# Softmax-weighted causal taps and a soft mixture of experts on one core: taps loaded to every row they need, logits steps and conv heads each in a row

## The chip, the core and the metric

The kernel runs on one core of one Trainium2 chip, in fp32. The metric is the device time of one execution in microseconds (us). The core has TensorE (PE; its weight loads are listed as PEld), VectorE (DVE), ScalarE (ACT), GpSimd (POOL), SyncE (SP, which issues nearly all transfers here) and 16 DMA engines. A name with a q (SPq, ACTq) is the queue of that engine.

## The reference, cut to what matters

```
w = softmax(weight, axis=-1)                   # 8 heads x 7 taps
x_pad = 6 zero rows before each of the 8 sequences of 3584 x 192
out[b,s,h*24:(h+1)*24] = sum_k w[h,k] * x_pad[b,s+k,h*24:(h+1)*24]
X = out.reshape(28672, 192)
logits = X @ phi                               # 32 slots: 8 experts x 4
d = softmax over the 28672 rows;  slot_in = d.T @ X
slot_out[e] = relu(slot_in[e] @ w1[e]) @ w2[e]   # 192 -> 1024 -> 192
c = softmax over the 32 slots;    result = c @ slot_out
```

## The kernel before, in words

**Batches and stages.** The 8 sequences ("batches" b0 to b7) go through in four units of two. `load_x(b)` brings a batch to one of five buffers (`rb0` to `rb4`) in nine transfers on SP's queue (L271, L275). Each buffer row block needs 8 halo rows copied inside the buffer (`halo`, L199, mostly on POOL). For b0 and b1 a quarter's halo is copied in two pieces, as it is for the last quarter of b2; otherwise a quarter is one copy. The buffer of b5, b6, b7 is that of b0, b1, b2, so their loads are added right behind `dispatch(0)`, `dispatch(1)`, `dispatch(2)`, which read it last.

**Conv.** `conv` multiplies a batch by banded matrices `toep`, one per head (L460). For b0 to b2 (below `NHB`) a batch goes in two halves of four calls with two heads each; from b3 on one call takes one head of the whole batch. Every call takes the next of four pairs of PSUM banks (`take`), skipping the two that `logits` holds, and is evicted into the buffer by ACT (L197), for even batches from b2 on by ACT or DVE. `turn` transposes 32 channels at a time on DVE (L504) into `xt`.

**Logits, dispatch.** `logits(unit)` is six `step`s (k = 0 to 5, L549), each reading the transposes k of both batches. `done` then adds the moves from PSUM on DVE (L575, a running minimum) and the exponentials on ACT (L590). `turn_d(b)` transposes the exponentials on PE (L615) and copies them back, and `dispatch(b)` (L640) adds the batch to the slot sums.

**End.** Slot inputs go through `w1` (L870) and `w2` (L912), the result `so` is gathered (L948, L951), and the outputs are multiplied out (L983), evicted (L197, L201) and stored (L1009). `rows(b)` (L667 to L684) makes the softmax over slots; its steps have priorities of 1000 and more and are fitted into gaps. The weights come in as 16 transfers for `w1` (half h=0 into `rb3`, behind `dispatch(3)`; half h=1 into `rb4`, behind `dispatch(4)`) and eight for `w2` (into `xt` and `rb0`), all on SP's queue (L296).

**Order.** Nothing runs in the order of the text. `Plan.order` simulates the engines with hand-set costs and priorities and then emits every engine's instructions in the order that it found; PE's steps carry `chain=True` and so keep the order in which they are added. `stage(b, s, between)` adds a batch's convs and takes a table of what is to be added ahead of which head. Before the change that table spread the logits steps and the `turn_d`s:

```python
    lead = (2, 1, 1, 2)
                ld = (3, 1, 1, 1) if j == 2 else lead
                for h, n in enumerate(ld):
                    between[h] = [lambda z=z: step(z) for z in range(k, k + n)]
            if s and j > 1:
                between = {0: [lambda: turn_d(prev[0])], 1: [lambda: turn_d(prev[1])], 2: [lambda: dispatch(prev[0])]}
            if b == B - 1:
                between.update({6: [lambda: box.extend(logits(unit)), lambda: box[0](0)], 7: [lambda: box[0](1)]})
```

**Start.** The 56 tap weights come to one row; a matmul with a row of ones (L346) spreads them to 128 rows in PSUM, DVE and ACT make the softmax, `tprod`, `tsum` and 16 small matmuls (`tmm`, L395) make the bands, and `tcp` (L405) copies them to `toep`. `warmup` (L337) and `filler` (L490) are matmuls whose results nobody reads.

Of the kernel before, what the change touches and what calls it, by code (L numbers as in the profile page):

```python
# [10 lines left out]
ALU = mybir.AluOpType  # L11
# [140 lines left out]
def tile_conv_softmoe(ctx: ExitStack, tc: tile.TileContext, x, weight, phi, w1, w2, out):  # L152
    nc = tc.nc
    P = 128
# [65 lines left out]
    dnx = sb("dnx", P, U, P)  # L220
    wb = sb("wb", P, H * KT)
    ident = sb("ident", P, P)
# [4 lines left out]
    acc = sb("acc", P, D)  # L227
    ones = acc[:, 0:P]
    dtot = sb("dtot", P, 1)
# [18 lines left out]
    odd2 = small[:, 6:8]  # L248
    wm, ws = small[:, 8 : 8 + H], small[:, 16 : 16 + H]
    hk = [[f"h{i}.{h}" for h in range(H)] for i in range(NR)]  # L250
# [5 lines left out]
    def load_x(b):  # L256
        i = b % NR
        pr = b * 10 - 30
        n = NU // NQ4

        def zero(e):
            nc.gpsimd.memset(rb[i][0 : 2 * HR, 0, :], 0.0)

        add(zero, {"POOL": 0.4}, writes=[f"z{i}"], after=allk(i) + [f"z{i}"], prio=pr)
        for q in range(NQ4):

            def fn(e, q=q):
# [12 lines left out]

            add(fn, {"DMA": n * P * D * 4 / 325e3 + {(0, 0): 0.6, (1, 1): 1.1}.get((b, q), 0)}, writes=[ldk[i][q]], after=hk[i] + [hak[i][q], hak2[i][q]], prio=pr)
            reads = [ldk[i][q]] + ([f"z{i}"] if q == 0 else [])
            if b < 2 or (b, q) == (2, 3):
                um = n * q + n // 2
                first = lambda e, q=q, um=um: halo(e, n * q, um)
                add(first, {"POOL": 0.75}, reads=reads, writes=[hak[i][q]], prio=pr)
                add(lambda e, q=q, um=um: halo(e, um, n * (q + 1)), {"ACT" if b == 0 and q < 2 else "POOL": 0.75}, reads=reads, writes=[hak2[i][q]], prio=pr)
            else:
                add(halo, {"POOL": 1.5}, reads=reads, writes=[hak[i][q]], prio=pr)
# [4 lines left out]
    def load_w(dst, src, nbytes, key, after, prio, depth=0, behind=None, first=False):  # L294
# [14 lines left out]
    wv = wb.rearrange("p (h k) -> p h k", k=KT)  # L309
    wrow = tap.rearrange("p h t -> p (h t)")[0:1, 0 : H * KT]  # L310
    add(
        lambda e: nc.scalar.dma_start(wrow, bass.AP(weight.tensor, 0, ap=[[0, 1], [1, H * KT]])),
        {"ACT": 2.4}, writes=["wrow"], prio=-100,
# [5 lines left out]
    def c0(e):  # L319
        nc.vector.memset(warm, 0.0)  # L320
        nc.scalar.activation(warm, warm, AF.Exp)
        make_identity(nc, ident)
        nc.gpsimd.memset(ones[0:1], 1.0)
        nc.gpsimd.memset(strip, 0.0)
# [9 lines left out]
    def warmup(n):  # L334
# [8 lines left out]

    warmup(1)
    add(
        lambda e: nc.tensor.matmul(prs[1][:, 0, 0 : H * KT], ones[0:1], wrow, start=True, stop=True),  # L346
        {"PE": 0.2}, reads=["wrow", "ident"], writes=["p1"], prio=-100, chain=True,
    )
    warmup(2)

    def w_max(e):
        wp = prs[1][:, 0, 0 : H * KT].rearrange("p (h k) -> p h k", k=KT)
        nc.vector.tensor_reduce(out=wm, in_=wp, axis=AX.X, op=ALU.max)
        nc.vector.tensor_tensor(out=wv, in0=wp, in1=wm.unsqueeze(2).broadcast_to((P, H, KT)), op=ALU.subtract)

    def w_norm(e):
        nc.vector.tensor_reduce(out=ws, in_=wv, axis=AX.X, op=ALU.add)
        nc.vector.tensor_scalar(out=ws, in0=ws, scalar1=1e-9, scalar2=None, op0=ALU.add)
        nc.vector.reciprocal(ws, ws)
        nc.vector.tensor_tensor(out=wv, in0=wv, in1=ws.unsqueeze(2).broadcast_to((P, H, KT)), op=ALU.mult)  # L360

    add(w_max, {"DVE": 0.5}, reads=["p1"], writes=["wb"], prio=-50)
    add(lambda e: nc.scalar.activation(wb, wb, AF.Exp), {"ACT": 0.25}, reads=["wb"], writes=["wb", "wexp"], prio=-50)
# [5 lines left out]
    add(w_norm, {"DVE": 0.9}, reads=["wb"], writes=["wb"], prio=-50)  # L369
    
    TB = 7
    KB = TB + KT - 1
    spread = dnx.rearrange("p u n -> p (u n)")[0:KB, 0 : H * TB * KT]

    def tprod(e):
        dst = spread.rearrange("p (h t k) -> p h t k", h=H, t=TB)
        eye = bass.AP(ident.tensor, ident.offset, ap=[[ident.ap[0][0], KB], [0, H], [1, TB], [1, KT]])
        nc.vector.tensor_tensor(out=dst, in0=eye, in1=wv[0:KB].unsqueeze(2).broadcast_to((KB, H, TB, KT)), op=ALU.mult)

# [5 lines left out]
    add(tprod, {"DVE": 0.45}, reads=["ident", "wb"], writes=["spread"], prio=-45)  # L385
    add(tsum, {"DVE": 0.45}, reads=["spread", "p1"], writes=["tap"], prio=-45)

# [28 lines left out]

    add(selector, {"DVE": 0.8}, reads=["ident"], writes=["gsel"], prio=1050)

# [4 lines left out]

    add(masks, {"DVE": 0.3}, reads=["ident"], writes=["mask"], prio=1050)

# [7 lines left out]

    add(row_parity, {"DVE": 0.6}, reads=["ident"], writes=["pmask"], prio=1051)

# [75 lines left out]
    def stage(b, s, between=()):  # L511
        between = dict(between)
        if b < NHB:
            spare = ((0, 0, 0, 4), (0, 0, 0, 1), (), (), (), ())
            for lo in (0, NI):
# [170 lines left out]
    for b in range(NR):  # L686
        load_x(b)
    lead = (2, 1, 1, 2)
    for j, unit in enumerate(units):
        prev = units[j - 1] if j else []  # L690
        for s, b in enumerate(unit):
# [4 lines left out]
            elif j == 1 and s == 0:  # L696
                for k in range(3):
                    lead0[0](k, 1)
                for k in range(3, NB):
                    lead0[0](k)  # L700
                lead0[1]()
                between = {
                    H: [lambda: state.update(held=())],
                    2 * H - 4: [lambda: turn_d(prev[0])],
                    2 * H - 2: [lambda: turn_d(prev[1])],
                }
            elif s == 0 and prev:
                step, done = logits(prev)
                k = 0
                ld = (3, 1, 1, 1) if j == 2 else lead  # L710
                for h, n in enumerate(ld):
                    between[h] = [lambda z=z: step(z) for z in range(k, k + n)]
                    k += n
                between[len(ld) - 1] += [done, lambda: dispatch(units[j - 2][1]), lambda: state.update(held=())]
            if s and j > 1:
                between = {0: [lambda: turn_d(prev[0])], 1: [lambda: turn_d(prev[1])], 2: [lambda: dispatch(prev[0])]}
            if b == B - 1:
                box = []
                between.update({6: [lambda: box.extend(logits(unit)), lambda: box[0](0)], 7: [lambda: box[0](1)]})
            stage(b, s, between)  # L720
            if b == 0:
                add(phi_copies, {"ACT": 1.05}, reads=["phi0", hk[0][6] + ".0"], writes=["phi4"], prio=12)
            if s == 0 and j == 1:
                dispatch(prev[0])
    step, done = box
    for k in range(2, NB):
        step(k)
# [317 lines left out]
```

## Time and profile before

| | |
|---|---|
| median of 3 runs | 200.6 us (200.0 to 201.22) |
| the profiled execution | 201.81 us, of which the span is 199.9 us |
| PE, DVE, ACT, POOL busy | 84%, 72%, 52%, 40% of the span |
| granted PE clock, mean | 0.93 |

The span begins with the first instruction and ends with the last transfer; 1.9 us of the execution lie around it. The profiled execution is 1.2 us above the median.

### The profile page before, as it was taken

To read this page: it belongs to the slowest core of one execution; us is meant where nothing else is said; L and a number is where in the kernel's file an instruction comes from. 1 tells how busy PE (TensorE), PEld (TensorE's weight loads), DVE (VectorE), ACT (ScalarE), POOL (GpSimd) and SP (SyncE) were. 2 spreads that over 40 slices of the span, in tenths; PEclk is the share of its full clock that TensorE was granted. 3 is DMA by queue.
4 is the path that set the end of the run, shared out by engine and by line. 5 is a ranking of instruction groups with operands and counts; after the bars stand their busy time and mean duration, and the time that the engine had idled before them with its cause. 6 is when DMAs were issued, how large, how long until landed. Compare 5 with 4: busy or idle time off the path is not lost.

```text
span 199.9 us, 6456 instructions
## 1 busy us (share of the span) xinstructions
PE 168.2 (84%) x2686; PEld 107.8 (54%) x2686; DVE 144.3 (72%) x242; ACT 104.7 (52%) x206; POOL 79.1 (40%) x79
## 2 busy tenths in 40 slices
PE   7996799989999999999999998997999998670000
PEld 3474646466434564355634584346999998660000
DVE  6568357579996989989999876588988998760000
ACT  3375343464924867428762450135999999560000
POOL 8364657556666056580004303327234345300000
PEclk9999699999999999999999999999999998867555
DMA  5999999999993899915897999920899999999994
GB/s 161 324 313 328 319 327 323 329 318 328 322 329 94 249 334 302 331 36 160 282 326 248 304 369 377 372 99 3 237 355 386 408 405 412 412 398 411 417 415 166
DMA packets 46767, 60.11 MB, mean 301 GB/s; under 512 B 2322, under 2 KB 39570, under 8 KB 46738
## 3 DMA queue, kind: packets, MB, share of 16 engines
q1 hardware_dynamic: 46528, 59.68, 88.7%
q8 instruction: 21, 0.34, 0.7%
q14 instruction: 8, 0.07, 0.1%
q10 hardware_dynamic: 210, 0.02, 0.1%
HBM read 37.68 MB, written 22.02 MB: 299 GB/s over the span
## 4 chain that ended last, share of the span: by engine, by line
PE 67%; DVE 7%; SPq 5%; DMA 4%; ACT 3%; issue 1%; POOL 0%; ACTq 0%; DVEq 0%
PE ps L460 20%; PE bk L983 16%; PE ps L549 13%; PE ps L640 10%; DMA rb<-in_x_dram 4%; SPq L275 4%; PE ps L615 4%; PE ps L870 3%; DVE rms L674 2%; ACT rb L197 2%; DVE eb L684 2%; ACT xt L590 1%; DVE eb L575 1%; DVE eb L677 1%; PE ps L897 1%
## 5 line engine op out<-in xcount | busy, mean ns | idle before, releaser
L504 DVE STREAM_TRANSPOSE xt<-rb 128x512 f32<-128x512 f32 (+1 forms) x66 | 58.1, 928 | 10.6 <-ACT rb L197 9.3
L199 POOL COPY rb<-rb 8x1536 f32<-8x1536 f32 (+1 forms) x39 | 46.6, 1197 | 36.2 <-DMA rb<-in_x_dram 33.4
L197 ACT COPY rb<-ps 128x768 f32<-128x768 f32 x57 | 43.0, 811 | 32.5 <-PE ps L460 29.2
L460 PE MATMUL ps<-rb,toep 64*64 64x192 f32 (+1 forms) x704 | 49.2, 415 | 3.5 <-POOL rb L199 2.8
L667 POOL TENSOR_TENSOR eb<-eb,rms 128x896 f32<-128x896 f32 x16 | 27.1, 1698 | 39.2 <-DVE rms L671 27.1
L983 PE MATMUL bk<-so,eb 32*128 32x192 f32 x448 | 38.9, 441 | 2.9 <-DVE eb L684 2.3
L983 PEld LDWEIGHTS bk<-so,eb 32*128 32x128 f32 x448 | 37.8, 317 | 3.7 <-issue 2.0
L460 PEld LDWEIGHTS ps<-rb,toep 64*64 64x64 f32 x704 | 25.4, 138 | 24.9 <-issue 12.8
L197 ACT COPY rb<-bk 128x384 f32<-128x384 f32 (+1 forms) x91 | 32.9, 505 | 5.3 <-PE bk L983 4.6
L549 PE MATMUL ps<-xt,phi 32*32 32x448 f32 x768 | 27.0, 544 | 0.1
L201 DVE COPY rb<-bk 128x384 f32<-128x384 f32 (+1 forms) x37 | 16.5, 490 | 4.1 <-PE bk L983 2.4
L549 PEld LDWEIGHTS ps<-xt,phi 32*32 32x32 f32 x768 | 10.3, 103 | 13.5 <-issue 6.8
L674 DVE TENSOR_REDUCE rms<-eb 128x28 f32<-128x896 f32 x16 | 17.1, 1069 | 0.5 <-ACT eb L680 0.5
L640 PE MATMUL ps<-rb,xt 128*32 128x192 f32 x320 | 13.8, 327 | 0.0
L590 ACT ACTIVATE xt<-eb,nmr 128x896 f32<-128x896 f32 x8 | 8.3, 1044 | 10.0 <-DVE eb L575 9.6
L640 PEld LDWEIGHTS ps<-rb,xt 128*32 128x32 f32 x320 | 10.0, 110 | 3.9 <-issue 1.2
L197 ACT COPY xt<-ps 128x512 f32<-128x512 f32 (+2 forms) x10 | 5.0, 517 | 9.5 <-DVE xt L201 8.6
L615 PE MATMUL ps<-ident,xt 128*128 128x128 f32 x64 | 8.7, 279 | 1.2 <-ACT rb L197 0.8
L615 PEld LDWEIGHTS ps<-ident,xt 128*128 128x128 f32 x64 | 6.9, 141 | 4.7 <-ACT xt L590 1.3
L684 DVE STREAM_TRANSPOSE eb<-eb 128x896 f32<-128x896 f32 x8 | 8.8, 1105 | 0.7 <-POOL eb L667 0.7
L677 DVE STREAM_TRANSPOSE eb<-eb 128x896 f32<-128x896 f32 x8 | 8.6, 1080 | 0.0
L640 PE MATMUL ps<-rb,dnx 128*32 128x192 f32 x192 | 8.4, 328 | 0.0
(98 smaller groups left out, 120.2 us busy)
## 6 DMA issues: line engine op xcount, KB each, us to landing
rb<-in_x_dram SPq DMA_DIRECT2D x56, 384.0 KB, 6.9
out_dram<-rb SPq DMA_DIRECT2D x28, 672.0 KB, 9.6
rb<-in_moe_w_dram SPq DMA_DIRECT2D x8, 512.0 KB, 4.8
xt<-in_moe_w_dram SPq DMA_DIRECT2D x4, 768.0 KB, 9.0
rb<-in_moe_w_dram SPq DMA_DIRECT2D x4, 768.0 KB, 12.0
rb<-in_x_dram SPq DMA_DIRECT2D x8, 288.0 KB, 6.1
rb<-in_moe_w_dram SPq DMA_DIRECT2D x8, 256.0 KB, 4.0
out_dram<-rb SPq DMA_DIRECT2D x4, 480.0 KB, 4.9
```

What stands on the lines that cost most here:

```text
L197: nc.scalar.copy(dst, src)
L199: nc.gpsimd.tensor_copy(dst, src)
L201: nc.vector.tensor_copy(dst, src)
L460: nc.tensor.matmul(dst[:, :, h * CG : (h + 1) * CG], toep[r, h0 + h, :], rb[i][r, lo + g : lo + n : 2, ch], start=True, stop=True,)
L504: nc.vector.transpose(xt[:, s, k, lo : lo + n], rb[i][:, lo : lo + n, 32 * k : 32 * k + 32])
L549: marks[f"L{unit[-1]}"] = nc.tensor.matmul(q[a % 2][32 * c : 32 * c + 32, a // 2, 0 : m * U * TH].rearrange("p (s u j) -> p s u j", s=m, j ...
L615: nc.tensor.transpose(q[:, u // 4, (u % 4) * P : (u % 4 + 1) * P], t[:, u].rearrange("p g t -> p (g t)"), ident)
L640: nc.tensor.matmul(q[32 * c : 32 * c + 32, 0, 0:D], d[:, u, 32 * c : 32 * c + 32], rb[i][:, U * c + u, :], start=(u == 0), stop=(u == U - 1),)
L667: return lambda e: veng(e).tensor_tensor(out=ev, in0=ev, in1=rb_, op=op)
L674: return lambda e: nc.vector.tensor_reduce(out=rm, in_=ev, axis=AX.X, op=op)
L684: add(lambda e: nc.vector.transpose(fl, fl), {"DVE": dve(NC)}, reads=ks, writes=[f"ct{b}"], prio=pr)
L983: nc.tensor.matmul(banks[own[c]][:, (q - k) * D : (q - k + 1) * D], cb[:, :, q], so[sl, :], start=True, stop=True, tile_position=(32 * c, 0),)
```

## The change

The tap weights are loaded to 13 rows at once, so the spreading matmul and its row of ones go, and the softmax works on 13 rows out of SBUF. The three warmups then stand in a row, and four fillers instead of one follow the second half of b0. Three small set-up steps on DVE wait for the bands. The last quarter of b3 gets its halo in two pieces. All six logits steps of a unit are added in a row; `dispatch` of the unit before's second batch follows them, and then the eight heads in a row. Both `turn_d`s stand ahead of the odd batch's heads (for unit 0: behind all of b2's), and `dispatch(prev[0])` behind that batch's heads.

```diff
-    wb = sb("wb", P, H * KT)
+    wb = sb("wb", P, H * KT)[0 : KT + 6]
-    ones = acc[:, 0:P]
...
-            if b < 2 or (b, q) == (2, 3):
+            if b < 2 or b < 4 and q == 3:
...
-    wrow = tap.rearrange("p h t -> p (h t)")[0:1, 0 : H * KT]
+    TB = 7
+    KB = TB + KT - 1
+    wrow = tap.rearrange("p h t -> p (h t)")[0:KB, 0 : H * KT]
     add(
-        lambda e: nc.scalar.dma_start(wrow, bass.AP(weight.tensor, 0, ap=[[0, 1], [1, H * KT]])),
+        lambda e: nc.scalar.dma_start(wrow, bass.AP(weight.tensor, 0, ap=[[0, KB], [1, H * KT]])),
...
-        nc.gpsimd.memset(ones[0:1], 1.0)
...
-    warmup(1)
-    add(
-        lambda e: nc.tensor.matmul(prs[1][:, 0, 0 : H * KT], ones[0:1], wrow, start=True, stop=True),
-        {"PE": 0.2}, reads=["wrow", "ident"], writes=["p1"], prio=-100, chain=True,
-    )
-    warmup(2)
+    warmup(3)
...
-    add(w_max, {"DVE": 0.5}, reads=["p1"], writes=["wb"], prio=-50)
+    add(w_max, {"DVE": 0.5}, reads=["wrow"], writes=["wb"], prio=-50)
...
-    add(selector, {"DVE": 0.8}, reads=["ident"], writes=["gsel"], prio=1050)
+    add(selector, {"DVE": 0.8}, reads=["ident", "toep7"], writes=["gsel"], prio=1050)
...
-            spare = ((0, 0, 0, 4), (0, 0, 0, 1), (), (), (), ())
+            spare = ((0, 0, 0, 4), (0, 0, 0, 4), (), (), (), ())
...
-                between = {
-                    H: [lambda: state.update(held=())],
-                    2 * H - 4: [lambda: turn_d(prev[0])],
-                    2 * H - 2: [lambda: turn_d(prev[1])],
-                }
+                between = {H: [lambda: state.update(held=())]}
             elif s == 0 and prev:
                 step, done = logits(prev)
-                k = 0
-                ld = (3, 1, 1, 1) if j == 2 else lead
-                for h, n in enumerate(ld):
-                    between[h] = [lambda z=z: step(z) for z in range(k, k + n)]
-                    k += n
-                between[len(ld) - 1] += [done, lambda: dispatch(units[j - 2][1]), lambda: state.update(held=())]
+                for k in range(NB):
+                    step(k)
+                done()
+                dispatch(units[j - 2][1])
+                state["held"] = ()
             if s and j > 1:
-                between = {0: [lambda: turn_d(prev[0])], 1: [lambda: turn_d(prev[1])], 2: [lambda: dispatch(prev[0])]}
-            if b == B - 1:
-                box = []
-                between.update({6: [lambda: box.extend(logits(unit)), lambda: box[0](0)], 7: [lambda: box[0](1)]})
+                between = {0: [lambda: turn_d(prev[0]), lambda: turn_d(prev[1])]}
             stage(b, s, between)
...
             if s == 0 and j == 1:
+                turn_d(prev[0])
+                turn_d(prev[1])
+            if j and s == (j > 1):
                 dispatch(prev[0])
-    step, done = box
-    for k in range(2, NB):
+    step, done = logits(unit)
+    for k in range(NB):
         step(k)
     done()
```

## Rows read from the trace of the kernel before

**Rows 1.** The page: 40 slices of 5 us; the chain's shares by engine.
```profile
PEclk9999699999999999999999999999999998867555
GB/s 161 324 313 328 319 327 323 329 318 328 322 329 94 249 334 302 331 36 160 282 326 248 304 369 377 372 99 3 237 355 386 408 405 412 412 398 411 417 415 166
...
PE 67%; DVE 7%; SPq 5%; DMA 4%; ACT 3%; issue 1%; POOL 0%; ACTq 0%; DVEq 0%
```
**Rows 2.** The chain in order of time: start us, us, what.
```profile
11.25 8.82 DMA rb<-in_x_dram
```
**Rows 3.** Timeline of PE to 25 us: start us, us, engine, line, operation, tile.
```profile
3.37 0.67 PE L346 MATMUL ps<-tap,acc 1*128 1x56 f32 x2
...
12.68 1.99 PE L490 MATMUL ps<-ident 128*128 128x256 f32 x8
...
17.46 0.70 PE L490 MATMUL ps<-ident 128*128 128x256 f32 x2
21.00 4.51 PE L460 MATMUL ps<-rb,toep 64*64 64x192 f32 x64 [2.84 <-POOL rb L199]
```
**Rows 4.** One window, all engines: us, busy by engine, PEclk, DMA share, GB/s.
```profile
22.00:23.00 1.00, 1.00 (x18) 0.84 (x16) 0.06 (x1) 0.80 (x1) 0.52 (x2) 0.50 1.11 300
```
**Rows 5.** Timeline of PE, the output stage.
```profile
167.28 4.86 PE L983 MATMUL bk<-so,eb 32*128 32x192 f32 x56 [0.64 <-DVE eb L684]
```
**Rows 6.** Timeline of PE, first logits steps to `dispatch(0)`.
```profile
25.44 2.48 PE L549 MATMUL ps<-xt,phi 32*32 32x448 f32 x48
27.85 1.53 PE L460 MATMUL ps<-rb,toep 64*64 64x192 f32 x32
...
42.32 1.03 PE L615 MATMUL ps<-ident,xt 128*128 128x128 f32 x8 [0.81 <-ACT rb L197]
...
45.93 2.81 PE L640 MATMUL ps<-rb,xt 128*32 128x192 f32 x64
```
**Rows 7.** Timeline of PE, b3 to the last logits step and `dispatch(5)`.
```profile
48.67 5.39 PE L460 MATMUL ps<-rb,toep 64*64 64x384 f32 x64
53.99 3.10 PE L549 MATMUL ps<-xt,phi 32*32 32x448 f32 x96
57.02 0.88 PE L460 MATMUL ps<-rb,toep 64*64 64x384 f32 x8
...
110.48 2.81 PE L640 MATMUL ps<-rb,dnx 128*32 128x192 f32 x64
```
**Rows 8.** Timeline of DVE, moves of unit 0 to the transposes of b3.
```profile
36.99 0.62 DVE L575 TENSOR_SCALAR_CACHE_REDUCE eb<-ps 128x448 f32<-128x448 f32 x1 [3.51 <-PE ps L549]
...
49.23 9.83 DVE L504 STREAM_TRANSPOSE xt<-rb 128x512 f32<-128x512 f32 x11
58.98 1.07 DVE L677 STREAM_TRANSPOSE eb<-eb 128x896 f32<-128x896 f32 x1
```
**Rows 9.** Timeline of POOL: last halo of b3, last halo of b7.
```profile
44.29 1.46 POOL L199 COPY rb<-rb 8x1536 f32<-8x1536 f32 x1 [1.27 <-DMA rb<-in_x_dram]
...
86.95 1.46 POOL L199 COPY rb<-rb 8x1536 f32<-8x1536 f32 x1 [0.71 <-DMA rb<-in_x_dram]
```
**Rows 10.** Timeline of SP's queue: load of b7, `w1` half h=1, output stores.
```profile
72.96 0.34 SPq L271 DMA_DIRECT2D rb<-in_x_dram  x1
...
100.40 1.84 SPq L296 DMA_DIRECT2D rb<-in_moe_w_dram  x3
...
139.18 49.33 SPq L1009 DMA_DIRECT2D out_dram<-rb  x36
```
**Rows 11.** End of the weight loads: one window of PE and DMA; PE's timeline.
```profile
131.00:132.00 1.00, 1.00 (x16) 1.00 0.37 138
...
133.91 0.49 PE L912 MATMUL ps<-xt 128*32 128x384 f32 x2
```
**Rows 12.** Timeline of ACT: the evictions of b3's eight heads.
```profile
49.65 5.72 ACT L197 COPY rb<-ps 128x768 f32<-128x768 f32 x8 [2.57 <-PE ps L460]
```
**Rows 13.** One window of the last stage, as in Rows 4.
```profile
180.00:190.00 10.00, 0.00 (x0) 0.00 (x0) 0.00 (x0) 0.00 (x0) 0.00 (x0) 0.60 1.02 412
```

More of the change, by code (lines that the diff above doesn't have):

```diff
@@ L248, in tile_conv_softmoe @@
     odd2 = small[:, 6:8]
-    wm, ws = small[:, 8 : 8 + H], small[:, 16 : 16 + H]
+    wm, ws = small[0 : KT + 6, 8 : 8 + H], small[0 : KT + 6, 16 : 16 + H]
     hk = [[f"h{i}.{h}" for h in range(H)] for i in range(NR)]
@@ L342, in warmup @@
             )
-    warmup(1)
-    add(
-        lambda e: nc.tensor.matmul(prs[1][:, 0, 0 : H * KT], ones[0:1], wrow, start=True, stop=True),
-        {"PE": 0.2}, reads=["wrow", "ident"], writes=["p1"], prio=-100, chain=True,
-    )
-    warmup(2)
+    warmup(3)
     def w_max(e):
-        wp = prs[1][:, 0, 0 : H * KT].rearrange("p (h k) -> p h k", k=KT)
+        wp = wrow.rearrange("p (h k) -> p h k", k=KT)
         nc.vector.tensor_reduce(out=wm, in_=wp, axis=AX.X, op=ALU.max)
-        nc.vector.tensor_tensor(out=wv, in0=wp, in1=wm.unsqueeze(2).broadcast_to((P, H, KT)), op=ALU.subtract)
+        nc.vector.tensor_tensor(out=wv, in0=wp, in1=wm.unsqueeze(2).broadcast_to((KB, H, KT)), op=ALU.subtract)
     def w_norm(e):
@@ L359, in w_norm @@
         nc.vector.reciprocal(ws, ws)
-        nc.vector.tensor_tensor(out=wv, in0=wv, in1=ws.unsqueeze(2).broadcast_to((P, H, KT)), op=ALU.mult)
-    add(w_max, {"DVE": 0.5}, reads=["p1"], writes=["wb"], prio=-50)
+        nc.vector.tensor_tensor(out=wv, in0=wv, in1=ws.unsqueeze(2).broadcast_to((KB, H, KT)), op=ALU.mult)
+    add(w_max, {"DVE": 0.5}, reads=["wrow"], writes=["wb"], prio=-50)
     add(lambda e: nc.scalar.activation(wb, wb, AF.Exp), {"ACT": 0.25}, reads=["wb"], writes=["wb", "wexp"], prio=-50)
@@ L377, in tprod @@
         eye = bass.AP(ident.tensor, ident.offset, ap=[[ident.ap[0][0], KB], [0, H], [1, TB], [1, KT]])
-        nc.vector.tensor_tensor(out=dst, in0=eye, in1=wv[0:KB].unsqueeze(2).broadcast_to((KB, H, TB, KT)), op=ALU.mult)
+        nc.vector.tensor_tensor(out=dst, in0=eye, in1=wv.unsqueeze(2).broadcast_to((KB, H, TB, KT)), op=ALU.mult)
     def tsum(e):
@@ L385, in tile_conv_softmoe @@
     add(tprod, {"DVE": 0.45}, reads=["ident", "wb"], writes=["spread"], prio=-45)
-    add(tsum, {"DVE": 0.45}, reads=["spread", "p1"], writes=["tap"], prio=-45)
+    add(tsum, {"DVE": 0.45}, reads=["spread"], writes=["tap"], prio=-45)
     def tmm(e):
@@ L422, in masks @@
             nc.vector.tensor_reduce(out=mask[:, a : a + 1], in_=src, axis=AX.XY, op=ALU.add)
-    add(masks, {"DVE": 0.3}, reads=["ident"], writes=["mask"], prio=1050)
+    add(masks, {"DVE": 0.3}, reads=["ident", "toep7"], writes=["mask"], prio=1050)
     def row_parity(e):
@@ L432, in row_parity @@
             )
-    add(row_parity, {"DVE": 0.6}, reads=["ident"], writes=["pmask"], prio=1051)
+    add(row_parity, {"DVE": 0.6}, reads=["ident", "toep7"], writes=["pmask"], prio=1051)
     state = {"pair": 0, "held": ()}
```

3 lines of the change are left out of this document (removed).

## The prediction, made before the changed kernel was built

> **What bounds the kernel now.** I read the chain first: PE holds 67% of it [rows 1]. Read in order of time it has three parts. To 21 us it is SP's issues and the landing of x: one piece of 8.82 us is nothing but b1's load [rows 2], and the conv of b1 starts at 21.00 behind the halo that waited for it [rows 3]. From 21 us to about 137 us it is PE. From then on it is the output: SP issues the stores from 139.18 on [rows 10], the transfers run at about 400 GB/s [rows 1], and between 180 and 190 us no engine computes while DMA is full at 412 GB/s [rows 13]. So the last part has a fixed length, as long as the outputs keep ahead of the queue, and whatever PE gains between 21 and 137 us arrives at the end. The second view is PE's timeline, which shows that PE hardly idles in that stretch but runs in three ways that cost: at half clock, waiting for ACT, and switching between kinds of matmuls. The third is DVE's timeline, which shows how little slack the transposes have behind it.
>
> **The change, part by part.** *Taps.* The spreading matmul (0.67 us [rows 3]) and a memset go. The bands are ready some tenths earlier, and that is worth nothing: the b1 load holds the chain until 21.00 whatever happens before it [rows 2, 3]. The same load covers the three set-up steps on DVE that move behind the bands, and the three more fillers: four fillers took 1.99 us and one 0.70 [rows 3], so PE ends at 17.46 + 1.99 = 19.45 instead of 18.16, still ahead of 21.00. Price of all this: nothing.
>
> *Clock at 21 us.* Before, PE sat idle for 2.84 us and then ran the four conv calls of b1's first half in 4.51 us [rows 3], at a granted clock of 0.50, which is 1.2 GHz [rows 4]. The slice 20 to 25 us is the only one before the output stage that shows less than 9 tenths [rows 1]. The fillers cut the idle time to 21.00 - 19.45 = 1.55 us. The trace has gaps on both sides of it: after 0.81 us at 41.5 us the clock stayed [rows 1, 6], after 0.64 us at 166.6 us it fell [rows 1, 5], but that was among matmuls on 32 of the 128 rows, and here the gap follows fillers on all 128 [rows 3, 5]. I take it that the clock holds. Then the four calls take about 2 x 1.53 = 3.06 us [rows 6] and end at 24.06; the three half logits steps behind them took 27.85 - 25.44 = 2.41 [rows 6], so b1's second half starts at about 26.45 instead of 27.85. That is 1.4 us; bounds 0 (the clock falls as before) and 1.45 (all that the four calls lose, 4.51 - 3.06).
>
> *b2 and `turn_d`.* Before, PE waited 0.81 us at 41.5 us for the exponentials and an eviction, then ran turn_d, a call, turn_d, a call, and reached `dispatch(0)` at 45.93: 4.42 us [rows 6]. With both calls first nothing waits for the exponentials: two calls at 1.53 / 2 and two turns at 1.03 [rows 6] are 3.59 us. Gain 0.8; bounds 0 (the calls wait for banks that ACT, busy with exponentials, has not emptied) and 0.8.
>
> *Rows of steps and heads.* A head alone between other matmuls takes 0.88 us, eight in a row 5.39, or 0.67 each [rows 7]. From 53.99 to 110.48 PE does 18 logits steps, 32 heads (b4 to b7), four turns and four dispatches, in 56.49 us [rows 7]. In a row, three steps cost 57.02 - 53.99 = 3.03, eight heads 53.99 - 48.67 = 5.32, a dispatch 48.67 - 45.93 = 2.74 [rows 6, 7], a turn 1.03. New sum: 6 x 3.03 + 4 x 5.32 + 4 x 2.74 + 4 x 1.03 = 54.54. Gain 1.95; bounds 0 (each row waits elsewhere for as much) and 1.95.
>
> Together 1.4 + 0.8 + 1.95 = 4.15 us. What is late next takes some of it back:
>
> *Transposes ahead of logits(2,3).* DVE goes from the first move at 36.99 to the end of b3's transposes at 49.23 + 9.83 = 59.06: 22.07 us [rows 8]. Starting 1.4 earlier it ends at 57.65. PE would start the six steps at 53.99 - 2.2 = 51.8 and come to the last one, which needs b3's last transpose, five steps (5.05) later, at 56.85. So the last step waits 0.8 us at most; 0 if DVE loses the waits that it had in this stretch. I take 0.4. Before, three heads lay between the steps and hid this. In the later units a dispatch (2.74) now stands between the odd batch's heads and the logits, and gives DVE that time.
>
> *Weights.* `dispatch(4)` now ends six steps (6.06) before the last logits end. The SP queue holds `w1` half h=1 behind it, and `w2` behind that. Before, h=1 began at 100.40 and the stream ended at about 131.4 [rows 10, 11]: 31.0 us. The last quarter of `w2` is needed at 133.91 [rows 11], 23.43 after the logits ended at 110.48 [rows 7]. At the same pace it lands 31.0 - 6.06 = 24.94 after: 1.5 us late. At the rate of the slices from 115 to 130 us, 369 to 377 GB/s [rows 1], the 9.4 MB of h=1 and `w2` need 25.4 us and come in time. Half h=0 can now start once `dispatch(3)` is done, at about 85 (the sum of the next paragraph), and is out of the way when h=1 begins, so I take 0.5, from bounds of 0 and 1.5.
>
> *Loads and halos.* `dispatch(2)` now comes behind b5's heads, and b7's load waits for it. It starts at 51.8 + 6.06 + 2.74 + 5.32 + 2.06 + 5.32 = 73.3 (steps, dispatch, b4's heads, turns, b5's heads), about where the load began before, at 72.96 [rows 10]. Load and halos then took to 86.95 + 1.46 = 88.4 [rows 9], 15.5 us, so to about 89 now. A dispatch, six steps and `dispatch(3)` bring PE to 84.8, b6's heads and two turns to 92.2, where b7's conv starts: hidden by 3 us. b3's conv would start at 48.67 - 2.2 = 46.5 [rows 7]; its last halo ended at 44.29 + 1.46 = 45.75 [rows 9], and the piece split off only brings it forward: hidden.
>
> *Evictions.* ACT took 5.72 us for the eight heads of b3 [rows 12], 0.05 us per head more than PE's 0.67 [rows 7]. PE did not wait for it in that row, since four pairs of banks let ACT fall some heads behind, and the turns and dispatches between rows let it catch up: 0; upper bound 32 x 0.05 = 1.6. The Trainium skill (TensorEngine Tiling (Array Packing), PSUM Bottleneck) says that tiling speeds up TensorE but not the emptying of PSUM, which may then be the bottleneck. It speaks against heads in a row; by it the 1.6 us would be lost, and the row of b3, eight heads without a wait, does not show it.
>
> The sum: 201.81 - 4.15 + 0.4 + 0.5 = 198.56 for the profiled execution; it stood 1.2 above the median, so a median of 200.6 - 3.25, about **197.3 us**.
>
> **The rivals.** *The clock falls anyway*, and the extra fillers don't do what they seem to be there for. The idle time of 1.55 us remains, and 0.64 us was once enough [rows 5]; against it stands the 0.81 us that was not. Gain 3.25 - 1.4 = 1.85: 198.8.
>
> *The weight stream is the bound* at its old pace: another 1.0 us is lost, 198.3. For it: SP issues in order and h=1 starts late against the logits. Against it: the free DMA time that h=0 leaves.
>
> *Evictions set the pace of the rows*: 1.6 us lost, 198.9. For it the 5.72 us, against it b3's row.
>
> *A filled-in step ahead of the transposes* (the other side). Each logits row now needs its last transpose within six steps of its start. DVE's order is fixed by the plan, and a step of `rows(b)` such as L677 takes 1.07 us [rows 8]. One of them ahead of the last transposes in each of the three rows costs 3 x 1.07 = 3.2: 200.5, no change. Two in each, 6.4: 203.7. It is slower from 1.4 us of wait per row on. For it: DVE has no slack in the first row. Against it: at 58.98 the step came behind b3's last transpose [rows 8], because the plan fits such steps only into gaps that it sees.
>
> **How the numbers follow.** Forecast 0.52 (its own range 196.0 to 198.8: the 4.15 us whole with nothing taken back is 196.45, with both waits at their upper bounds 198.75, and the runs shown spread by 0.6 to either side), clock 0.15, weights 0.06, evictions 0.05, one step 0.11, two steps 0.11. A difference of 0.5%, 1 us, is about what a measurement here can tell from none. Faster: 0.52 + 0.15 + 0.06 + 0.05 = 0.78. Same: 0.11. Slower: 0.11. The range reaches from 195.8 (196.45 less that spread) up to 200.7, where the case of one step lies, and leaves out the slower one and a little below.
>
> **What would show it.** Right: PEclk at 9 tenths in the slice 20 to 25 us and b1's second half at about 26.45; `dispatch(0)` at about 43.7; six steps of 1.01 us with no wait but the last in the first row; the last logits end at about 107; `so` and the first store some 3.3 us earlier, at about 136; the same length from there. Wrong: a gap on PE in front of a logits step that DVE's transposes end (the last rival), a wait of L912 for a transfer (the stream), conv heads more than 0.7 us apart with ACT busy (evictions), or a longer way from first store to end, which would mean that the outputs, not the queue, set the last part.

## The result and the profile after

| | before | after |
|---|---|---|
| median, timed together | 200.0 us (198.34 to 201.56, 21 runs) | 202.7 us (200.2 to 205.76, 21 runs) |
| ratio | | 1.009, 95% interval 1.0064 to 1.0116 |
| profiled execution, span | 201.81, 199.9 us | 200.57, 198.8 us |

The ratio uses only the executions within 1.5% of the fastest of their kernel (14 of the 21 of after), and the medians hold all of them. So the change costs 0.9%, some 1.8 us, where 3.3 us of gain were forecast; 202.7 also lies above the range of the forecast, which ended at 200.7. The profiled execution of after is one of its fastest, and that of before was slower than all its 21 runs, so the pair of profiles alone would mislead.

The page of after, slices and chain as in [rows 1], with one line of its part on DMA queues:

```profile
PEclk9999999999999999999999999999997899678555
GB/s 164 330 323 327 324 326 323 332 322 332 320 331 264 332 106 160 298 237 249 284 86 237 342 385 374 370 168 3 244 356 378 417 404 410 415 404 403 416 420 183
...
q8 instruction: 21, 0.34, 0.7%
...
PE 55%; DMA 14%; DVE 11%; ACT 3%; SPq 3%; issue 3%; POOL 2%; ACTq 0%; POOLq 0%
```

The slice of 20 to 25 us is at 9 tenths now. But PE has lost share of the chain to DMA (4% to 14%) and DVE (7% to 11%), and "issue", time in which an engine waits for nothing that the profile shows, has gone from 1% to 3%. PE's timeline of after, answering to [rows 3, 6, 7, 11]:

```profile
19.68 2.83 PE L452 MATMUL ps<-rb,toep 64*64 64x192 f32 x64
...
24.85 1.53 PE L452 MATMUL ps<-rb,toep 64*64 64x192 f32 x32
...
32.83 1.04 PE L541 MATMUL ps<-xt,phi 32*32 32x448 f32 x31 [0.17 <-issue]
33.80 1.53 PE L452 MATMUL ps<-rb,toep 64*64 64x192 f32 x32
...
38.80 1.84 PE L452 MATMUL ps<-rb,toep 64*64 64x192 f32 x34 [0.27 <-issue]
...
42.60 2.81 PE L632 MATMUL ps<-rb,xt 128*32 128x192 f32 x64
45.34 5.39 PE L452 MATMUL ps<-rb,toep 64*64 64x384 f32 x64
51.18 6.59 PE L541 MATMUL ps<-xt,phi 32*32 32x448 f32 x192 [0.45 <-DVE xt L496]
57.70 0.84 PE L632 MATMUL ps<-rb,dnx 128*32 128x192 f32 x11
58.84 2.47 PE L632 MATMUL ps<-rb,dnx 128*32 128x192 f32 x53 [0.30 <-issue]
61.24 5.39 PE L452 MATMUL ps<-rb,toep 64*64 64x384 f32 x64
...
76.52 5.94 PE L541 MATMUL ps<-xt,phi 32*32 32x448 f32 x192
82.39 2.47 PE L632 MATMUL ps<-rb,dnx 128*32 128x192 f32 x53
86.16 0.84 PE L632 MATMUL ps<-rb,dnx 128*32 128x192 f32 x11 [1.30 <-issue]
86.93 5.39 PE L452 MATMUL ps<-rb,toep 64*64 64x384 f32 x64
...
108.10 2.81 PE L632 MATMUL ps<-rb,dnx 128*32 128x192 f32 x64
...
133.14 0.52 PE L898 MATMUL ps<-rb,xt 128*32 128x384 f32 x2 [0.76 <-DMA rb<-in_moe_w_dram]
...
135.08 0.94 PE L934 MATMUL ps<-xt 128*128 128x192 f32 x4 [0.46 <-DVE xt L201]
```

Two things are new. In the middle of `dispatch(1)` and of `dispatch(3)` PE stops for 0.30 and 1.30 us, and for 0.17 and 0.27 us earlier on. From start to the next operation's start these dispatches take 61.24 - 57.70 = 3.54 and 86.93 - 82.39 = 4.54 us, against 2.74 before. And `w2`'s matmuls (L898) wait for the weights. SP's queue and the chain of after show why (first fence SP, as in [rows 10]; second the chain, as in [rows 2]):

```profile
74.37 0.34 SPq L270 DMA_DIRECT2D rb<-in_x_dram  x1
...
102.37 9.44 SPq L295 DMA_DIRECT2D rb<-in_moe_w_dram  x8
...
138.40 50.27 SPq L995 DMA_DIRECT2D out_dram<-rb  x36
```

```profile
121.17 11.92 DMA rb<-in_moe_w_dram
```

Half h=1 of `w1` is issued when `dispatch(4)`, now behind all heads of b7, has ended. ACT, answering to [rows 12]:

```profile
46.33 5.72 ACT L197 COPY rb<-ps 128x768 f32<-128x768 f32 x8 [2.77 <-PE ps L452]
```

For the comparisons below every trace is cut at three starts in PE's timeline: b3's conv (45.34 in after), `dispatch(5)` behind the last logits (108.10), and the gather behind `w2` (135.08). All in us; the names are those of the experiments.

| kernel | b3's conv at | to `dispatch(5)` | to the gather | to the end of the span | span |
|---|---|---|---|---|---|
| before [rows 7] | 48.67 | 61.81 | 25.38 | 64.04 | 199.9 |
| before, again (e8) | 45.50 | 62.50 | 26.76 | 63.34 | 198.1 |
| after | 45.34 | 62.76 | 26.98 | 63.72 | 198.8 |
| after, again (e4) | 46.12 | 61.86 | 28.19 | 63.83 | 200.0 |
| e1, `dispatch(4)` back | 45.17 | 62.38 | 25.80 | 63.75 | 197.1 |
| e11, before, no late x | 45.42 | 62.34 | 25.73 | 64.11 | 197.6 |
| e10, after, no late x | 46.04 | 60.16 | 28.72 | 64.08 | 199.0 |
| e13, e10 and e1 together | 45.55 | 60.32 | 25.40 | 64.03 | 195.3 |

Where `dispatch(4)` stands behind b7's heads (after, e4, e10), a shorter second stretch goes with a longer third. Of all kernels with the changed order only e13 is short in both. The kernel before is not the same in its two executions either: e8 reaches `dispatch(5)` at 108.00, as early as after.

### The profile page after: what moved, and what is told of

Read it like the earlier page. It is cut to its first block, busy times and chain, and to the rows that moved or that the text cites. A ratio compares the mean times of both kernels' runs of the same rounds, so it can differ in the third digit from the quotient of the medians.

```text
span 198.8 us, 6465 instructions
## 1 busy us (share of the span) xinstructions
PE 166.3 (84%) x2690; PEld 111.9 (56%) x2690; DVE 144.5 (73%) x244; ACT 102.3 (51%) x204; POOL 79.1 (40%) x79
## 4 chain that ended last, share of the span: by engine, by line
PE 55%; DMA 14%; DVE 11%; ACT 3%; SPq 3%; issue 3%; POOL 2%; ACTq 0%; POOLq 0%
PE ps L452 18%; PE ps L632 11%; PE ps L541 10%; PE bk L969 10%; DMA rb<-in_moe_w_dram 6%; DVE xt L496 5%; DMA out_dram<-rb 4%; DMA rb<-in_x_dram 4%; PE ps L607 3%; SPq L274 3%; ACT rb L197 2%; DVE rb L201 2%; POOL eb L659 2%; DVE eb L567 1%; DVE rms L666 1%
## 5 line engine op out<-in xcount | busy, mean ns | idle before, releaser
L496 DVE STREAM_TRANSPOSE xt<-rb 128x512 f32<-128x512 f32 (+1 forms) x66 | 57.2, 922 | 5.7 <-ACT rb L197 5.7
L197 ACT COPY rb<-ps 128x768 f32<-128x768 f32 x55 | 40.2, 833 | 20.0 <-PE ps L452 14.5
L452 PE MATMUL ps<-rb,toep 64*64 64x192 f32 (+1 forms) x704 | 44.8, 399 | 2.8 <-ACT rb L197 2.4
L969 PE MATMUL bk<-so,eb 32*128 32x192 f32 x448 | 39.6, 451 | 3.9 <-DVE eb L676 1.9
L969 PEld LDWEIGHTS bk<-so,eb 32*128 32x128 f32 x448 | 38.5, 318 | 4.9 <-issue 2.1
L541 PE MATMUL ps<-xt,phi 32*32 32x448 f32 x768 | 26.2, 544 | 0.9 <-DVE xt L496 0.5
L541 PEld LDWEIGHTS ps<-xt,phi 32*32 32x32 f32 x768 | 12.0, 103 | 13.0 <-DVE xt L496 5.4
L632 PE MATMUL ps<-rb,dnx 128*32 128x192 f32 x192 | 9.4, 328 | 1.6 <-issue 1.6
L632 PEld LDWEIGHTS ps<-rb,dnx 128*32 128x32 f32 x192 | 6.1, 109 | 6.0 <-issue 4.5
L201 DVE COPY rb<-ps 128x768 f32<-128x768 f32 x9 | 8.3, 954 | 1.2 <-PE ps L452 0.5
```

The source lines that it names most:

```text
L197: nc.scalar.copy(dst, src)
L201: nc.vector.tensor_copy(dst, src)
L452: nc.tensor.matmul(dst[:, :, h * CG : (h + 1) * CG], toep[r, h0 + h, :], rb[i][r, lo + g : lo + n : 2, ch], start=True, stop=True,)
L496: nc.vector.transpose(xt[:, s, k, lo : lo + n], rb[i][:, lo : lo + n, 32 * k : 32 * k + 32])
L541: marks[f"L{unit[-1]}"] = nc.tensor.matmul(q[a % 2][32 * c : 32 * c + 32, a // 2, 0 : m * U * TH].rearrange("p (s u j) -> p s u j", s=m, j ...
L632: nc.tensor.matmul(q[32 * c : 32 * c + 32, 0, 0:D], d[:, u, 32 * c : 32 * c + 32], rb[i][:, U * c + u, :], start=(u == 0), stop=(u == U - 1),)
```

## The experiments

**e1: `dispatch(4)` back among b7's heads.** In the changed kernel:

```diff
             if s and j > 1:
                 between = {0: [lambda: turn_d(prev[0]), lambda: turn_d(prev[1])]}
+                if j == 3:
+                    between[2] = [lambda: dispatch(prev[0])]
...
-            if j and s == (j > 1):
+            if j and s == (j > 1) and not (s and j == 3):
                 dispatch(prev[0])
```

> The changed kernel, with dispatch(4) alone put back ahead of b7's third head (as before the change), so that w1 half h=1 is released earlier. Weight theory (the late release of h=1 makes the w2 stream the bound and swallows the gain): the 0.76 us wait of the w2 matmuls for a transfer is gone, so comes 1.2 us or more earlier, the median 1.5 to 2.5 us below the changed kernel's. Theory of PE's unexplained stalls (1.3 and 0.3 us inside dispatch(3) and dispatch(1)): nothing changes, same time within 0.5 us. Transposes theory: slower than the changed kernel by up to 1 us, since b7's last transposes lose the cover of the dispatch.

Measured 200.69 us (198.72 to 202.13), ratio 1.0009 (0.9972 to 1.0046). No matmul of `w2` waits for a weight; the gather comes 25.80 us behind `dispatch(5)`, where after and e4 need 26.98 and 28.19. Windows of PE and DMA (as in [rows 4]), first after, then e1, show the transfers that moved:

```profile
100.00:102.00 2.00, 2.00 (x57) 1.54 (x48) 2.00 (x3) 2.00 (x3) 0.00 (x0) 1.00 0.08 31
102.00:104.00 2.00, 2.00 (x74) 1.03 (x68) 2.00 (x4) 0.21 (x1) 0.00 (x0) 1.00 0.16 45
```

```profile
100.00:102.00 2.00, 2.00 (x40) 0.80 (x48) 2.00 (x3) 2.00 (x4) 0.00 (x0) 1.00 0.92 236
102.00:104.00 2.00, 2.00 (x84) 1.22 (x66) 2.00 (x2) 0.88 (x2) 0.00 (x0) 1.00 0.64 244
```

DMA lies nearly idle for 4 us in after (31 and 45 GB/s) and not in e1. So the place of `dispatch(4)` costs most of the loss, but giving it back leaves a kernel that is as fast as before, not faster.

**e2: the taps alone; e3: the rows alone.** e2 has the changed start (13 rows by DMA, fillers, set-up steps, b3's halo) and the loop over batches of the kernel before; e3 the other way round.

> The first part alone: taps by DMA, three warmups in a row, four fillers, late set-up steps and the split halo of b3, with the steps and heads interleaved as before. If the taps part holds the clock and the rows part loses: faster than before by 1.5 to 2.5 us. If the taps part is worth nothing: 200.0 within 0.5 us. If the taps part is what makes the changed kernel slow: slower than before by 1 us or more.

> The second part alone: logits steps and heads in rows, turns and dispatches moved, with the old taps and one filler. If the rows lose through the weight stream: slower than before by 1 to 3 us, with a wait of the w2 matmuls for a transfer in the trace. If the rows gain 1 to 2 us by themselves, as forecast: faster than before by as much. The clock falls at 21 us as before in both cases.

e2: 200.32 us, ratio 1.0008 (0.9978 to 1.0037). e3: 202.19 us, ratio 1.0091 (1.0055 to 1.0127). The whole loss is in the rows; the taps give nothing. The conv of b1's first half in e3, which has the one filler of before:

```profile
20.33 2.83 PE L460 MATMUL ps<-rb,toep 64*64 64x192 f32 x64 [1.99 <-POOL rb L199]
```

It takes 2.83 us, and not the 4.51 of [rows 3], without the added fillers; the granted clock between 20 and 25 us is 1.00 (2.4 GHz), where [rows 4] has 0.50.

**e4: the changed kernel again.**

> The changed kernel unaltered, for a second trace and more times. Its single times went from 200.2 to 205.8. Weight theory: the trace of a slower execution shows a longer wait of the w2 matmuls for a transfer, and the rest of the chain as in the first trace. Rival: the stretch from the first store to the end is longer instead (60.4 us in the first trace). Rival: PE's stalls within the dispatches are longer.

201.94 us, ratio 1.0096 (1.0059 to 1.0133). Its waits at the weights are longer than those in the profile of after:

```profile
132.38 0.84 PE L898 MATMUL ps<-xt 128*32 128x384 f32 x4 [0.71 <-DMA xt<-in_moe_w_dram]
...
134.23 0.52 PE L898 MATMUL ps<-rb,xt 128*32 128x384 f32 x2 [1.01 <-DMA rb<-in_moe_w_dram]
```

**e5, e6, e7: half of `w2`'s transfers left out** of the changed kernel, of e1 and of the kernel before (the second layer uses the other half's weights twice):

```diff
         def fn(e):
+            if key.startswith("w2.") and key.endswith(".0"):
+                return
             ins = nc.sync.dma_start(dst, src).ins
...
```

> The changed kernel with half of w2 never loaded (the four transfers into xt are left out and the second layer reads the other four experts' weights twice); every engine's order is that of the changed kernel. Weight theory: the w2 matmuls wait for nothing, so and the first store come 1.5 to 2.5 us earlier, and the median falls by as much, to about 200.3; the spread of single times shrinks from 5 us to about 3. Rival (the loss lies elsewhere): the median falls by less than 0.5 us.

> The kernel with dispatch(4) put back, and half of w2 not loaded in the same way. Its profiled execution took 198.9 us but its median was 200.7. If its slower executions are those in which w2 is late even so: the median falls by 1 us or more, to below 199.7. If they are late for another reason: within 0.5 us of 200.7.

> The kernel before, with half of w2 not loaded in the same way. Weight theory: before the change the stream ended 2.5 us ahead of need, so nothing changes: 200.0 within 0.5 us. If the stream already set the end in many executions before: faster by 1 us or more.

e5: 201.88 us (197.5 to 205.17), ratio 0.9956 (0.9905 to 1.0007); e6: 202.33 (199.38 to 203.71), 1.0114 (1.0058 to 1.017); e7: 200.28, 1.0006 (0.9977 to 1.0035). In the traces the waits for weights are gone as expected (26.03, 25.40 and 25.37 us from `dispatch(5)` to the gather), but the times don't follow: median and ratio of e5 disagree (its twelve times are spread over 7.7 us), and e6, of six times, is slower than e1, which has more to load. The theory of the weights alone fell here. What e5's trace, that of an execution of 202.06 us, shows beside them are three gaps of PE that end with "issue", 3.0 us together:

```profile
34.72 1.04 PE L543 MATMUL ps<-xt,phi 32*32 32x448 f32 x31 [0.66 <-issue]
...
60.67 2.47 PE L634 MATMUL ps<-rb,dnx 128*32 128x192 f32 x53 [0.79 <-issue]
...
88.24 0.84 PE L634 MATMUL ps<-rb,dnx 128*32 128x192 f32 x11 [1.56 <-issue]
```

Added up from the first line of the timeline, 473, 979 and 1485 of PE's records stand ahead of these gaps. In after the gaps stand behind 473, 598, 979 and 1485, so always at the same places, and these are 125, 381 and 506 apart: 1, 3 and 4 times about 126.5.

**e8: the kernel before again, with a profile.**

> The kernel before unaltered, for a second trace. The first trace lost 1.4 us to a low clock at 21 us. If that is what the kernel usually does: the conv of b1's first half takes about 4.5 us again. If that trace was an exception, as the rows-only run suggests (one filler, 1.99 us idle, no fall): 2.83 us, with PEclk at 1.00.

200.04 us. The conv of b1's first half:

```profile
19.67 2.83 PE L460 MATMUL ps<-rb,toep 64*64 64x192 f32 x64 [1.23 <-POOL rb L199]
```

The granted clock is 1.00 (2.4 GHz) from 20 to 25 us. Of the traces of this code the fall of the clock in [rows 3, 4] belongs to that one execution, which also had the longest idle time ahead of the conv (2.84 us; 1.99 in e3, 1.23 here). There is no gap with "issue" in this trace, as there was none in the first one; e7 has one of 0.48 us. But `w2` waits for its weights in the kernel before, too:

```profile
132.82 0.52 PE L912 MATMUL ps<-rb,xt 128*32 128x384 f32 x2 [0.57 <-DMA rb<-in_moe_w_dram]
```

The gather comes 26.76 us behind `dispatch(5)`, against 25.38 in the first trace. So a late stream is not new with the change.

**e9: 24 records more in front.** Each warm-up matmul of 512 columns is given as four of 128:

```diff
-            add(
-                lambda e: nc.tensor.matmul(
-                    prs[0][:, 0, :].rearrange("p (r n) -> p r n", n=P), ident, ident.unsqueeze(1).broadcast_to((P, 4, P)),
...
+            def four(e):
+                for r in range(4):
+                    nc.tensor.matmul(prs[0][:, 0, P * r : P * r + P], ident, ident, start=True, stop=True)
+
+            add(four, {"PE": 1.3}, reads=["ident"], writes=["p0"], prio=-100, chain=True)
```

> The changed kernel, with each of TensorE's warm-up matmuls of 512 columns given as four of 128 (24 records more ahead of the first convolution, the same columns; nothing else differs). Theory of the instruction supply: the gaps that end with nothing that the profile shows stand behind the 473rd, 598th, 979th and 1485th record of TensorE in every trace of this kernel that has them, all about a multiple of 126.5 apart, because a packet of the instruction queue (21 packets, 0.34 MB) holds so many; 24 records more ahead of them put the largest, in the dispatch behind the logits of batches 4 and 5, behind 29 of its 64 records instead of 53, and the one in the dispatch behind the logits of 2 and 3 out of that dispatch, some 13 records ahead of the end of those logits. The time stays within 0.5% of the changed kernel (201.5 to 203 us). Rival, a wait of that very instruction (a buffer or a semaphore that the profile does not name): the gaps stay behind 53 and 11 records of the same dispatches.

202.98 us (202.5 to 203.36), ratio 1.0121 (1.0072 to 1.017), and the profile:

```profile
86.18 1.82 PE L630 MATMUL ps<-rb,dnx 128*32 128x192 f32 x35 [1.15 <-issue]
```

35 of the 64 records of `dispatch(3)` come after the gap, so 29 ahead of it: 24 fewer than the 53 of after, and 1485 from the start as before. The other one has left `dispatch(1)`, which is clean (2.74 us), for the row of steps ahead of it, which takes 7.58 us instead of 6.52. The gap belongs to a place in PE's instruction stream, not to an operation. The page gives 21 packets and 0.34 MB for the instruction queue q8, and PE has 2690 matmuls and as many weight loads: 5380 / 21 = 256 to a packet, 128 pairs, which fits the distance. The Trainium skill (Runtime: NRT & Kernel Launch, Instruction fetch mechanics) says that instructions are fetched by DMA in blocks of 256, and that the cost of crossing a block is mostly hidden. The size agrees with the 256; that it is hidden does not hold here, where a crossing costs up to 1.30 us in after, and the measurement decides.

**e10 and e11: no input in flight.** The changed kernel and the kernel before without the input transfers of b5 to b7, whose convs then work on what the buffers held:

```diff
+                if b >= NR:
+                    return
                 u0, base = n * q, b * S - 2 * HR
```

> The changed kernel without the input transfers of batches 5 to 7 (their convolutions and transposes read what the three buffers held before; everything else is issued as in the changed kernel). Theory of the instruction supply: with no input in flight from about 47 us on, the instruction packets land at once, and the gaps behind the 979th and the 1485th record (0.3 to 0.8 and 0.6 to 1.6 us) are gone; the late weights are left as they are, or come earlier since the queue is free. The time comes down to about 200 us (199 to 201), and the ratio to the kernel before falls from 1.009 to within 0.5% of 1.00. Rival, the gaps belong to the order of the rows and not to the transfers: they stay at 0.6 us or more together, and the time stays at 201.5 or above.

> The kernel before, without the same input transfers of batches 5 to 7. Theory of the instruction supply: the kernel before has next to no such gaps in its traces (one of 0.48 us in three), so only the waits for these transfers can go: 199 to 200.3 us, ratio 0.995 to 1.00, no gap. If the input transfers hold back both kernels alike, this one falls by as much as the changed one (1.5 us or more), and the theory does not explain the difference between them.

e10: 201.24 us, ratio 1.0035 (1.0 to 1.0071). e11: 199.25, ratio 0.9945 (0.9914 to 0.9977). There is no gap in e10's trace. `dispatch(3)` there, and the windows of the same time in e10 and after:

```profile
82.29 2.81 PE L634 MATMUL ps<-rb,dnx 128*32 128x192 f32 x64
85.02 5.39 PE L454 MATMUL ps<-rb,toep 64*64 64x384 f32 x64
```

```profile
80.00:82.00 2.00, 2.00 (x83) 1.16 (x58) 1.95 (x2) 0.00 (x0) 2.00 (x2) 1.00 0.03 8
82.00:84.00 2.00, 2.00 (x55) 1.38 (x48) 1.47 (x5) 0.02 (x1) 1.91 (x2) 1.00 0.00 0
84.00:86.00 2.00, 2.00 (x40) 1.10 (x36) 1.63 (x5) 1.84 (x4) 0.07 (x1) 1.00 0.03 8
```

```profile
80.00:82.00 2.00, 2.00 (x89) 1.24 (x60) 2.00 (x3) 0.00 (x0) 1.45 (x1) 1.00 0.99 300
82.00:84.00 2.00, 2.00 (x57) 1.32 (x44) 1.43 (x5) 0.00 (x0) 0.00 (x0) 1.00 0.98 289
84.00:86.00 2.00, 0.86 (x21) 0.38 (x12) 1.39 (x4) 1.76 (x4) 1.21 (x1) 1.00 1.04 345
```

In e10 almost nothing moves but packets of this size (8 GB/s over 2 us are 16 KB), and PE is busy throughout. In after DMA is full with b7's load, and PE is busy for 0.86 of 2 us. The packets themselves can be seen in the part on DMA queues when it is asked for short windows. PE passes the place one packet (126 records) ahead of the 1485th record at 79.8 us in after and at 79.7 in e10 (counted from the records). In after q8 brings nothing between 80.0 and 83.7 us, while the data queue q1 takes 96.5% of the 16 engines; a packet comes between 83.7 and 84.8 (first line), and PE goes on at 86.16. In e10 it comes between 80.4 and 81.5 (second line):

```profile
q8 instruction: 1, 0.02, 5.6%
```

```profile
q8 instruction: 1, 0.02, 5.4%
```

5.6% and 5.4% of 16 engines over 1.1 us are both about 1.0 us. So the packet moves as fast in after as in e10, but it starts 3.9 us behind the place and not 0.7. That it stands behind data for that time is inferred from the full engines.

The stretch to `dispatch(5)` is 2.60 us shorter in e10, and that is the two dispatches, (3.54 - 2.74) + (4.54 - 2.73) = 2.61. But the wait for the weights grows: 28.72 us to the gather, against 26.98. Half h=1 is issued sooner in e10 (100.46; 102.37 in after), since `dispatch(4)` ends sooner, yet the last weight packet ends at 132.4 us, against 132.7. From that issue to the last packet are 32.0 us in e10, 30.3 in after and 31.5 in e4, the same kernel as after. What makes that length differ is not shown.

The two times do not show what the gaps cost, either: e10 falls by 0.55% (from 1.009) and e11 by 0.55%. So leaving out these inputs helps both kernels alike, as the rival put down for e11 says, though by 1.1 us and not by 1.5. In e11 it is the weights that come sooner (25.73 us to the gather, against the 26.76 of e8).

**e12: `dispatch(2)` and `dispatch(4)` back**, as e1 with `j in (2, 3)`.

> The changed kernel with the dispatches of batches 2 and 4 both put back between the heads of batches 5 and 7, where the kernel before has them (the experiment with dispatch of batch 4 alone gave 200.69 us, ratio 1.001). The load of batch 7 is then issued about 3.5 us sooner (near 70.5 us instead of 74.4) and is through the queue before the 1485th record. Theory of the instruction supply: the gap there falls below 0.4 us (0.77 and 1.03 in the two traces with only batch 4's put back), the chain to the last logits is 0.3 to 0.8 us shorter, and the time is 199.3 to 200.5 us, ratio 0.994 to 1.001. Rival, the order within the stage is all that counts: the gap stays at 0.8 to 1.0 us and the time at 200.5 to 201.2, for the added change of shape among the heads.

199.91 us, ratio 0.9989 (0.9955 to 1.0022): the fastest of the changed kernels with all the work, and not to be told from before. b7's load is issued at 70.05, 4.3 us sooner, but the gap does not shrink as expected. The load now overlaps the packet ahead of it, and PE stops in the row of steps, which takes 7.45 us instead of 5.87:

```profile
80.85 2.90 PE L541 MATMUL ps<-xt,phi 32*32 32x448 f32 x75 [0.68 <-issue]
```

**e13: both costs out**, e1 without the late inputs.

> The changed kernel without the input transfers of batches 5 to 7 and with the dispatch of batch 4 put back: both of the found costs are out. Theory (instruction supply plus late weights explain the whole difference, and the rows themselves gain what was worked out): no gap, no wait for a weight transfer, and the stretch from the end of batch 3's convolution to the last logits is 54.8 to 55.3 us as without the late inputs; the time is 197 to 198.3 us, 1 to 2 us below the kernel before without the same transfers (199.25, ratio 0.9945). Rival, a third cost is still hidden in the rows or in the order of the output stage: 198.8 us or more.

197.61 us (197.26 to 199.12), ratio 0.9864 (0.9822 to 0.9906), 1.6 us (0.8% by the ratios) below e11. No gap, no wait for a weight. The effects don't add: against the 1.009 of the change, e1 gives back 0.8%, e10 0.55%, both together 2.3%. This is where the gaps show in the time: with `dispatch(4)` back, the missing inputs are worth 1.45% (e1 to e13), to the kernel before 0.55% (e11); the 0.9% between, about 1.8 us, agree with the 62.38 - 60.32 = 2.06 us by which the second stretch is shorter. PE gains from the missing gaps only if the weights are there when it comes, and of the changed order e13 alone has both.

**e14: the rows cut in two**, on top of e12, to spread PE's records:

```diff
-                for k in range(NB):
+                for k in range(3):
                     step(k)
-                done()
-                dispatch(units[j - 2][1])
-                state["held"] = ()
+                between = {
+                    3: [lambda: dispatch(units[j - 2][1])],
+                    5: [lambda z=z: step(z) for z in range(3, NB)] + [done, lambda: state.update(held=())],
+                }
```

> The changed kernel with the dispatches of batches 2 and 4 put back, and the row of six logits steps of batches 2 and 3, and of 4 and 5, cut in two: three steps, three heads, the dispatch, two heads, three steps, three heads. No 126 records of TensorE then pass in under 5.2 us (4.7 and 3.9 us in the row). Theory of the instruction supply: the gaps shrink to 0.3 us or less together; the additional changes of shape cost 0.2 us each, some three in a unit, and batch 3's last transposes have three heads more of time (0.45 us of wait and 0.65 of slower logits before): 198.3 to 199.8 us, ratio 0.990 to 0.999. Rival, the added changes of shape and the halves of PSUM that the logits hold for longer cost as much as the gaps: 199.9 to 201 us.

206.65 us, ratio 1.0266 (1.0217 to 1.0315). The gaps are gone, as forecast, and much more is lost elsewhere: twice a head behind the steps waits for the moves out of the logits' banks, which the dispatch behind `done` had covered, and the first heads of b4 come ahead of their halo.

```profile
55.93 1.52 PE L452 MATMUL ps<-rb,toep 64*64 64x384 f32 x16 [1.82 <-POOL rb L199]
...
68.20 2.25 PE L452 MATMUL ps<-rb,toep 64*64 64x384 f32 x24 [2.31 <-DVE eb L567]
...
95.71 2.25 PE L452 MATMUL ps<-rb,toep 64*64 64x384 f32 x24 [2.31 <-DVE eb L567]
```

## Why the prediction was wrong

Two terms of the sum failed in the changed kernel itself: the late weights, which make it slower than the kernel before (e1 gives 0.8% back), and the rows of steps and heads, whose gain the gaps take (e1 is no faster than before, e13 is). A third, the clock, was never there to be gained.

**Taps**: nothing, as forecast (e2).

**Clock at 21 us**: the step that took 1.4 us off failed. The clock holds in after, but it holds in e8 and e3 as well, with one filler. The 1.4 us were a feature of one execution, and since the forecast also took off the 1.2 us by which that execution stood above the median, it probably counted the same thing twice.

**b2 and `turn_d`**: 0.8 forecast. From the start of b2's conv to `dispatch(0)` e8 takes 42.76 - 33.62 = 9.14 us, after 42.60 - 33.80 = 8.80, e12 42.56 - 34.35 = 8.21. So 0.3 to 0.9 is left, less where a gap falls into it. But the wait of 0.81 us that was to go is not in every execution of the kernel before: e7 takes 42.12 - 33.80 = 8.32 us and e11 42.68 - 34.20 = 8.48, no more than some of the changed order. A gain here is likely, and its size is not shown.

**Rows of steps and heads**: the gain of 1.95 is the step that failed here, since nothing was taken off it for PE's supply of instructions. The forecast for the stretch from b3's heads to the last logits was 54.54 + 0.4 = 54.94 us. With no input in flight it is that: 60.16 - 5.32 = 54.84 in e10. In after it is 62.76 - 5.32 = 57.44, and the 2.6 us between are the two stretched dispatches. "Each row waits elsewhere for as much" stood in the text as a bound of the gain, without a mechanism behind it: PE passes 126 records of such a row in 4 to 5 us, sooner than the next instruction packet lands while inputs stream (in after PE goes on 6.3 us behind the place one packet ahead of the gap).

**Transposes ahead of logits(2,3)**: 0.4 forecast, measured 0.45 ahead of the row and 6.52 - 5.87 = 0.65 within it. Most of it is made up by the steps, which take 5.87 / 6 = 0.98 in a row and not 1.01, and by the turns (1.90 / 2 = 0.95 and not 1.03).

**Weights**: 0.5 forecast from 0 to 1.5. In after the last wait ends at 133.14, 25.04 us behind the last logits, where 23.43 were allowed: 1.6 us late, and e4 (28.19 - 25.40 = 2.8) went past the bound. The step that failed here is the reading of when the old stream ended. The forecast took 131.4, but the trace of before still moves weights in the next window:

```profile
132.00:133.00 1.00, 1.00 (x20) 1.00 0.03 9
```

The last packet ends at 132.4, 32.0 us behind 100.40 and not 31.0; in after and e8 the wait ends 0.5 us behind the last packet. So about 1.0 us of slack was left in before (an estimate: 133.91 - 132.4 - 0.5), and not the 133.91 - 131.4 = 2.5 that the forecast started from. The stream did run faster in after, as argued (30.3 us), and was late all the same. That the 24.94 of the old pace and the 25.04 agree is luck. Forecast and rivals also took the stream's lateness for fixed: its length differs between executions (30.3, 31.5 and 32.0 us in after, e4 and e10), and in e8 it was late before the change.

**Loads, halos, evictions**: hidden as forecast. ACT took 5.72 us for b3's eight heads and no head waited for it. But the load of b7, issued from 74.37 instead of 72.96 [rows 10], now lies on the instruction packet that `dispatch(3)` needs; before, DMA was down to 36 GB/s between 85 and 90 us [rows 1], where PE passes that place.

**The last part**: 63.3 to 64.1 us from the gather to the end in all of the table: fixed, as forecast.

The sum: the forecast was -3.25 us, the ratio says +1.8. Between them lie the clock (1.4), the gaps (2.6 in after), the weights (1.1 more than forecast in after, 2.3 in e4) and up to 0.5 at b2, 5.1 to 6.8 us for the 5.05 that are missing. This adds up single traces, and by e8 a part of the weights' term is in the kernel before as well. e13, with the gaps and the late weights out, stands at 197.6, but without three loads; against e11, which lacks the same loads, 1.6 us are gained.

**Open**: why e6 is slower than e1 although its one profile shows less to wait for; and whether the wide spread of the changed kernel (200.2 to 205.76) is that of the gaps. Their sums with "issue" run from 1.15 to 3.0 us in the profiles of the changed order (after, e3, e4, e5, e9), which would fit, but so few profiles do not show it. Open, too, is what sets the length of the weight stream.

## What to carry to other kernels

When many small matmuls are packed into a row, count instructions as well as time: where PE runs through a packet's worth of them faster than a packet lands beside the data transfers, the row stops, and a gap that stays at the same record count when work is added in front shows it. Look, before moving a step, at which transfers are queued behind it, and ask of a gain ahead of a load stream whether the stream is early enough to let it through. Profile the unchanged kernel twice before taking a clock or a wait in it for its normal state.

## What was not expected of the hardware

Instruction packets are not free beside data: a place in PE's stream that costs nothing with DMA idle (e10) cost 0.2 to 1.3 us in after with inputs at some 300 GB/s. A packet takes about 1 us to move in both; it is late because it starts late, 3.9 us behind the place one packet ahead of the 1485th record in after, 0.7 us in e10. Nor does PE go on at once: the four gaps of after end 1.3 to 1.6 us behind the end of a q8 packet (from the records of the queue).
